# One written order of tasks for all engines in a scan followed by a bilinear feed-forward block

## The chip, the cores and the metric

The kernel runs on one core of one Trainium2 chip. The metric is the time of one execution on the device in microseconds (us); a kernel's figure is the median of its runs. A core has TensorE (matrix products into PSUM, here PE, with PEld for loading its weights), VectorE (DVE), ScalarE (ACT), GpSimd (POOL) and SyncE (SP), which here issues all DMAs from one queue. PSUM has eight banks of 128 partitions x 512 float32.

## What is computed

Four batches, eight heads, 768 positions, head size 32, state size 16. A gated linear recurrence runs along the positions; its result, as 3072 rows of 256, goes through a bilinear feed-forward block with float64 weights:

```
cum = cumsum(log(a)) in the chunk;  L[i,j] = exp(cum[i]-cum[j]) for i >= j, else 0
y[i]  = sum_j (C[i].B[j]) L[i,j] x[j]  +  (C[i].state) exp(cum[i])
state = exp(cum[last]) state + sum_j exp(cum[last]-cum[j]) B[j] x[j]
out   = ((y @ w1) * (y @ w2)) @ w3 @ w_out        # w1, w2: 256x1024, w3: 1024x1024, w_out: 1024x256
```

## The kernel before

**Chunks and slabs.** The positions are cut into 16 chunks of 48; two chunks of all batches are a slab of 384 tokens, eight slabs in all. In a chunk, the 16 groups of two heads lie side by side, the two heads on partition halves 0 to 63 and 64 to 127; the first 16 rows of a half stand for the carried state, the other 48 for the positions.

**A chunk** (`chunk`, L286) has these steps, each in two halves of eight groups where a digit 0 or 1 follows: `D` (L298) forms the exponents cum[i]-cum[j] with the causal mask as one product of a constant `LD` and a table `RD`, whose rows hold cum as three bf16 parts; `E` (L304) takes exp on ScalarE into `R`; `B` (L309) multiplies B by the last decay on GpSimd; `CB` (L314) forms C.B as 32 products of 96x48 from six bf16 slots (three parts of B against three of C); `M` (L328) multiplies the two on VectorE; `Mx` (L333) multiplies `R` by x in 16 float32 products, which gives y and the new state in one PSUM bank `py`; `Z` (L345) transposes the state and copies it in four pieces into the next chunk's x tile; `hi`, `lo` (L360, L364) split y into two fp32r parts for the next products. Chunk c+1's `Mx` waits for chunk c's `Z`. `load_cum` (L260) fetches the parts of cum from DRAM, where `a.save` (L211) put them after clip, log, scan and three rounding steps. B and C of slabs 1 to 7 are split on ScalarE, VectorE and GpSimd (`split_slab`, L225), written to DRAM and read back slot by slot (`load_pack`, L249); slab 0 uses float32 blocks.

**Weights.** Each block of 128x512 float64 values is loaded (`.D`) into one of four buffers `st` and turned into float32 (`from_f64`, L384): `.A` scales the high words, `.Y` moves one byte per value, `.L` shifts and masks, `.S` shifts and merges. w1 and w2 (eight blocks, 512 columns wide each) are then split into a high and a low fp32r part by `.H` and `.P` (L424). w_out stays float32 (`wof`). w3 and w_out are multiplied into one 1024x256 matrix by float32 products (`w3_item`, L449, tasks `v0` to `v15`), whose result is split by `e` (L475).

**Slabs.** `up` (L487) makes one of eight 128-column pieces of both y @ w1 and y @ w2, two PSUM tiles, six fp32r products each (high-high, high-low, low-high, two halves of the 256 rows). `gate_a` copies the one out on ScalarE, `gate_b` multiplies the other in on VectorE, `gate_hi` and `gate_lo` (L513, L518) split the product on ScalarE and GpSimd. `down` (L523) multiplies 128 tokens by the combined matrix, 24 products; `store_a`, `store_b` copy and write it out.

**Order.** The string `PLAN` (L21) is the order of tasks from the beginning to the end of slab 1's `down`, and all instructions that it issues are kept in that order on their engine; `ON_VECTOR` and `ON_POOL` say which tasks leave ScalarE or VectorE, and `+n` are n filler products on zeros. From slab 2 on a loop (L607) issues the work, with chunk steps of the next slab between the ups, and there only the products keep their order (`mm`, L108). The tail is L633: three downs, copies and stores.

Of the kernel before, what the change touches and what calls it, by code (L numbers as in the profile page):

```python
# [45 lines left out]
ON_VECTOR = """
o0.A o1.Y o2.Y o3.A v0.A v0.Y v11.A v14.A v3.Y v5.A v7.Y v8.Y w0.H w1.Y w2.A w3.H w3.Y w4.A w5.H w6.A w6.H
""".split()
ON_POOL = "s1.rB s1.rC s2.rB".split()

@with_exitstack
def kernel(
# [34 lines left out]
    NGF = 11

    const = ctx.enter_context(tc.tile_pool(name="const", bufs=1))
    work = ctx.enter_context(tc.tile_pool(name="work", bufs=2))
    dram = ctx.enter_context(tc.tile_pool(name="dram", bufs=1, space=bass.MemoryType.DRAM))
    ps_at = ctx.enter_context(tc.tile_pool(name="ps_at", bufs=4, space=bass.MemoryType.PSUM))
    ps_l = ctx.enter_context(tc.tile_pool(name="ps_l", bufs=1, space=bass.MemoryType.PSUM))  # L100


    ordered = [True]

    def ins(i):
        return tc.keep_in_program_order(i) if ordered[0] else i

    def mm(*args, **kw):  # L108
        return tc.keep_in_program_order(nc.tensor.matmul(*args, **kw))  # L109

    def load(*args):
        return ins(nc.sync.dma_start(*args))

    def acopy(*args):
        return ins(nc.scalar.copy(*args))  # L115

    def vtt(*args):
        return ins(nc.vector.tensor_tensor(*args))  # L118

    def vcopy(*args):  # L120
        return ins(nc.vector.tensor_copy(*args))  # L121

    def ptt(*args):
        return ins(nc.gpsimd.tensor_tensor(*args))  # L124

    GF = const.tile([P, NGF, TOK], F32, name="gf")  # L130
    gf_turn = [0]

    def next_gf():
        gf_turn[0] += 1
        return GF[:, (gf_turn[0] - 1) % NGF]

    G8 = NB * HP // 2
    NK = 2 * CPS * 2
    first = GF.rearrange("p a s -> p (a s)")
    C0 = first[:, :NK * G8 * T].rearrange("p (k g t) -> p k g t", k=NK, g=G8)  # L140
    B0 = first[:, NK * G8 * T:NK * (G8 * T + TE)].rearrange("p (k m) -> p k m", k=NK)
    zero = const.tile([P, 512], BF16, name="zero")
    nc.vector.memset(zero, 0.0)
    BN = [const.tile([P, CPS, NB * HP, N], F32, name=f"bn{i}") for i in range(2)]

    NG = NB * HP
    RI, RJ = T, T + 6
    KD = RJ + 3 * NG  # L150
    LD = const.tile([KD, 2, TE], BF16, name="ld")
    RD = const.tile([KD, NG, T], BF16, name="rd")
    ldc = const.tile([KD, 2, TE], F32, name="ldc")
    rdc = const.tile([KD, T], F32, name="rdc")
    rdg = const.tile([KD, NG], F32, name="rdg")
    XE = [const.tile([P, NB * HP, 2 * D], F32, name=f"xe{i}") for i in range(2)]

    NSLOT = 6
    KS = NSLOT * N
    BP = const.tile([KS, NB * HP, CPS, 2, TE], BF16, name="bp")  # L160
    CP = const.tile([KS, NB * HP, CPS, 2, T], BF16, name="cp")


    Q, SQ = P // (NB * H), a.shape[1]
    arkc = work.tile([P, 3, SQ], F32, name="arkc", tag="g", bufs=FT + 1)
    ar, keep, cum = [arkc[:, i] for i in range(3)]
    ct = GF[:, NGF - 1].bitcast(BF16)[:, :3 * SQ].rearrange("p (t s) -> p t s", t=3)
    cd = dram.tile([Q, 2, NG, 3, SQ], BF16, name="cd")

# [8 lines left out]
    @task("k.p")  # L178
    def _():
        def fill(t, pattern, op, value, base, step):  # L180
            ins(nc.gpsimd.affine_select(out=t, in_=t, pattern=pattern, compare_op=op, fill=value, base=base,
                                        channel_multiplier=step))

        ins(nc.gpsimd.memset(keep, 1.0))
        ins(nc.gpsimd.memset(keep.rearrange("p (c t) -> p c t", t=T)[:, :, 0:1], 0.0))
        ins(nc.gpsimd.memset(ldc, 0.0))
        for h2 in range(2):
            fill(ldc[:, h2], [[-1, TE]], ALU.is_ge, -BIG, N, 1)
            fill(ldc[:, h2], [[0, TE]], ALU.is_ge, 1.0, RI + 3 * h2 - 1, -1)
# [5 lines left out]
        fill(rdg, [[3, NG]], ALU.is_ge, 0.0, RJ + 2, -1)

    task("k.C")(lambda: ins(nc.gpsimd.memset(C0, 0.0)))
    task("k.X0")(lambda: ins(nc.gpsimd.memset(XE[0], 0.0)))
    task("k.X1")(lambda: ins(nc.gpsimd.memset(XE[1], 0.0)))
    task("k.L")(lambda: vcopy(LD, ldc))  # L200
    task("k.R")(lambda: vtt(RD, rdc.unsqueeze(1).broadcast_to([KD, NG, T]), rdg.unsqueeze(2).broadcast_to([KD, NG, T]),
                            ALU.add))
    task("a")(lambda: load(ar, a))
    task("a.clip")(lambda: ins(nc.vector.tensor_scalar(ar, ar, 1e-6, 1.0, ALU.max, ALU.min)))
    task("a.ln")(lambda: ins(nc.scalar.activation(ar, ar, AF.Ln)))
    task("a.scan")(lambda: ins(nc.vector.tensor_tensor_scan(cum, keep, ar, 0.0, ALU.mult, ALU.add)))
# [79 lines left out]
    def chunk(c):  # L286
# [59 lines left out]
        def _():  # L346
            if c + 1 == NCH:
                return
# [357 lines left out]
```

## Time and profile before

| | |
|---|---|
| Runs | 325.22, 324.51, 322.70 us; median 324.51 |
| Span of the profiled execution, first to last instruction | 323.5 us (its own time is not given apart from this; the runs stand at -0.8 to +1.7 us from the span) |
| Busy: PE, DVE, ACT, POOL | 92%, 48%, 46%, 36% of the span |
| Mean granted clock of TensorE | 0.968 |
| DMA | 45.31 MB, 26255 packets, of them 7600 under 512 B |
| First `up` | 40.87 us |

The page gives busy times of the engines and 40 slices of the span with busy tenths, granted clock (PEclk, tenths of full speed) and DMA. A group is one kind of instruction: line, engine, operation, written tile <- read tiles, shape, count, then busy time in us, mean ns of one, and the engine's idle time ahead of it with what ended it. A timeline row begins with its start and length in us. Windows give, for a stretch, the busy times of PE, PEld, DVE, ACT and POOL, then clock, DMA share and GB/s. Products of float32 operands appear as two records each.

### The profile page before, as it was taken

The page shows a single profiled execution, that of the slowest core. Times are in us where ns is not written, and L with a number is a line of the kernel's source. Part 1 is how long each engine was busy: PE and PEld are TensorE (multiplying, and loading weights), DVE is VectorE, ACT ScalarE, POOL GpSimd, SP SyncE. Part 2 cuts the span into 40 slices and gives each one's busy share as a digit, 9 for nine tenths or more (in the row PEclk, how much of TensorE's full clock was granted, in tenths as well). Part 3 has the DMA queues.
Part 4 walks back from the last instruction along what each step waited for, and adds up shares of the span by engine and source line. Part 5 has one row for each costly group of instructions (what it writes and reads, how often), then busy time and mean ns, then how long its engine had stood idle before and what let it go on. Part 6 is the DMA issues. An engine that isn't in the chain of part 4 may idle for free. (4 is left out here: it accounts for less than half of the span.)

```text
span 323.5 us, 6505 instructions
## 1 busy us (share of the span) xinstructions
PE 297.9 (92%) x2523; PEld 266.0 (82%) x2523; DVE 156.1 (48%) x288; ACT 147.9 (46%) x279; POOL 117.5 (36%) x142
## 2 busy tenths in 40 slices
PE   8695697887997799899999999999999999999995
PEld 3452587776996599799899999999989999999995
DVE  2879969688871632456331651256035405411210
ACT  4366696677671653343523441453145324422430
POOL 8027358415223272333522341342134304421430
PEclk9899699799999799799999999999999999999999
DMA  7599599997999676844581177129402930001001
GB/s 212 181 307 291 163 272 184 280 243 224 335 207 253 195 138 182 227 140 110 118 156 35 51 151 129 29 54 190 95 21 56 187 79 5 3 16 34 0 4 46
DMA packets 26255, 45.31 MB, mean 140 GB/s; under 512 B 7600, under 2 KB 17200, under 8 KB 25552
## 3 DMA queue, kind: packets, MB, share of 16 engines
q1 hardware_dynamic: 26224, 44.89, 54.3%
q8 instruction: 20, 0.33, 0.4%
q14 instruction: 11, 0.09, 0.1%
HBM read 36.77 MB, written 8.11 MB: 139 GB/s over the span
## 5 line engine op out<-in xcount | busy, mean ns | idle before, releaser
L124 POOL TENSOR_TENSOR g<-gf,g 128x384 fp32r<-128x384 f32 x64 | 66.2, 1037 | 98.0 <-ACT g L115 98.0
L109 PE MATMUL bank<-woh,g 128*128 128x256 f32 x384 | 75.3, 291 | 3.1 <-DVE wol L118 2.2
L118 DVE TENSOR_TENSOR gf<-gf,bank 128x384 f32<-128x384 f32 x48 | 26.5, 552 | 103.6 <-PE bank L109 100.7
L109 PEld LDWEIGHTS bank<-woh,g 128*128 128x128 f32 x384 | 62.4, 196 | 5.1 <-DVE wol L118 2.9
L115 ACT COPY gf<-bank 128x384 f32<-128x384 f32 (+1 forms) x72 | 31.7, 444 | 58.7 <-PE bank L109 50.5
L115 ACT CAST g<-gf 128x384 fp32r<-128x384 f32 x64 | 32.9, 514 | 54.7 <-DVE gf L118 51.7
L109 PE MATMUL bank<-wol,g 128*128 128x256 f32 x192 | 55.2, 287 | 0.0
L109 PE MATMUL bank<-xT,w1h 128*128 128x384 f32 x192 | 52.8, 355 | 0.1
L109 PE MATMUL bank<-xT,w2h 128*128 128x384 f32 x192 | 48.8, 335 | 0.0
L109 PEld LDWEIGHTS bank<-wol,g 128*128 128x128 f32 x192 | 37.6, 196 | 0.0
L109 PE MATMUL bank<-wof,mag 128*128 128x256 f32 x128 | 33.0, 410 | 2.6 <-DVE wof L420 2.6
L109 PEld LDWEIGHTS bank<-xT,w1h 128*128 128x128 f32 x192 | 33.1, 188 | 2.1 <-DVE xT L118 0.4
L109 PEld LDWEIGHTS bank<-xT,w2h 128*128 128x128 f32 x192 | 34.8, 188 | 0.0
L109 PE MATMUL bank<-xT,w1l 128*128 128x384 f32 x96 | 32.2, 335 | 0.0
L109 PE MATMUL bank<-xT,w2l 128*128 128x384 f32 x96 | 32.2, 335 | 0.0
L109 PEld LDWEIGHTS bank<-wof,mag 128*128 128x128 f32 x128 | 25.9, 206 | 7.3 <-DVE wof L420 3.0
L115 ACT COPY st<-st 128x512 uint8<-128x512 uint8 x20 | 27.4, 1370 | 7.6 <-DVE mag L402 7.4
L124 POOL TENSOR_TENSOR R<-bn,R 128x128 f32<-128x128 f32 x32 | 14.7, 478 | 43.3 <-issue 36.5
L124 POOL TENSOR_TENSOR part<-raw,part 128x512 bf16<-128x512 f32 (+1 forms) x14 | 15.9, 1137 | 33.3 <-ACT part L115 33.3
L121 DVE COPY xe<-Z 16x256 f32<-16x256 f32 x60 | 26.8, 447 | 1.1
L109 PEld LDWEIGHTS py<-R,xe 128*64 128x64 f32 x512 | 17.8, 146 | 11.4 <-DVE R L118 4.4
L115 ACT CAST part<-raw 128x512 bf16<-128x512 f32 (+1 forms) x28 | 16.0, 578 | 24.3 <-DMA raw<-in_Bt_dram 10.9
(69 smaller groups left out, 388.7 us busy)
## 6 DMA issues: line engine op xcount, KB each, us to landing
st<-in_w3t_dram SPq DMA_DIRECT2D x16, 512.0 KB
xe<-in_x_dram SPq DMA_DIRECT2D x32, 192.0 KB
st<-in_w_dram SPq DMA_DIRECT2D x8, 512.0 KB
db<-part SPq DMA_DIRECT2D x7, 384.0 KB
bp<-db SPq DMA_DIRECT2D x7, 384.0 KB
st<-in_w_out_dram SPq DMA_DIRECT2D x4, 512.0 KB
bn<-in_Bn_dram SPq DMA_DIRECT2D x8, 256.0 KB
dc<-part SPq DMA_DIRECT2D x7, 288.0 KB
```

What stands on the lines that cost most here:

```text
L109: return tc.keep_in_program_order(nc.tensor.matmul(*args, **kw))
L115: return ins(nc.scalar.copy(*args))
L118: return ins(nc.vector.tensor_tensor(*args))
L121: return ins(nc.vector.tensor_copy(*args))
L124: return ins(nc.gpsimd.tensor_tensor(*args))
```

## The change

Nearly the whole body is rewritten; what is computed stays.

- **Order.** `PLAN` now covers the whole kernel. Each word names a task, its engine (`:S` ScalarE, `:V` VectorE, `:G` GpSimd) and its PSUM banks (`@7,6`); every instruction, loads and stores too, keeps this order on its engine. The loop from slab 2 on is gone. The list has its first up right after the second chunk, runs all eight of slabs 0, 1 and 2 and four of slab 3 while w3 arrives, and has the first down (`d0.2.m`) after the last w3 product. Unsplit products of 28 ups wait in a ring `GS`.
- **Decays.** Chunks 0 and 1: log a is also loaded transposed (`at`), spread over a triangle (`Y0`, `Y1`) and multiplied in with one more float32 product per half, no trip through DRAM. Chunks 2 to 7: as before, with cum as two fp32r parts instead of three bf16. Chunks 8 to 15: no product; cum is loaded broadcast over the partitions (`K`, 393 KB), and `F` and `G` on VectorE or GpSimd subtract cum[j] and add the mask.
- **C.B.** B and C come as float32 blocks laid out on the host, two groups side by side (`bc`, 459 KB per chunk); eight float32 products of K=64, 128x96 on alternating row halves and two banks take the place of 32 bf16 ones, and splitting, writing and reading back the parts is gone.
- **Weights.** w1 and w2 blocks hold 128 columns of both matrices with all 256 rows (eight blocks, 1 KB runs in DRAM), so one block serves one `up`. `.Y` moves 16 bits per value. w_out and w3 blocks are also split by `.H` and `.P`, and w3 @ w_out is made of three fp32r products in place of a float32 one. These split tiles share the space of the ring `FR` of split gates (11 places).
- **Splitting of gates** (`h`, `l`) happens after w3 is done, on ScalarE or VectorE and VectorE or GpSimd by the list. The state copies `Z` go to three engines. x is loaded for all 128 partitions with zero rows (512 KB), so that nothing need be cleared.

Cut to its core (the list shown at its start, around the last w3 product, and at its end):

```diff
-ON_VECTOR = """
-ON_POOL = "s1.rB s1.rC s2.rB".split()
+k.act:S k.zero:V k.rd:G c0.B +7@5 a.D t.D k.tri:G k.R:V w0.D c0.N c1.B c1.N c1.X c0.CB@0,1 k.keep:G c0.X a.clip:V k.ld:G a.ln:S w1.D t.clip:V +1@7
...
+c1.lo:V w1.S:V l0.0.m@7,6 w1.H:S w4.D w5.A:S w1.P:V l0.0.a:S w5.Y:V l0.1.m@2,5 w5.L:V c2.N w7.A:V w5.S:V w7.Y:S l0.0.g:V l0.1.a:S w5.H:S w7.L:V w2.D
...
+l3.7.a:S v16.M@2,5 l3.7.g:V l3.5.m@3,4 c11.F0:V c11.F1:G l3.5.a:S c11.G0:G v17.M@2,5 l3.5.g:V c11.G1:V l3.6.m@0,6 e11.a:S@5 l0.2.h:V l0.3.h:V
+e10.a:S@2 l0.0.h:V e11.b:V@5 l0.3.l:G l0.1.h:S e10.b:V@2 l0.5.h:S l0.0.l:G l0.6.h:S l3.0.m@7,1 l0.7.h:S l1.4.h:S l0.4.h:V l0.1.l:V l1.6.h:S l0.5.l:V
...
+l7.1.m@7,4 l7.6.g:V l7.6.h:S l7.1.a:S l7.6.l:G l7.1.g:V l7.1.h:V l7.1.l:V d7.1.m@0 d7.2.m@1 d7.1.y:S d7.1.x d7.0.m@6 d7.2.y:V d7.2.x d7.0.y:S d7.0.x
+    NGS, NST, NMAG, NFR, NOB, NCT, NR, NPK = 28, 4, 5, 11, 2, 2, 2, 3
+    pin = tc.keep_in_program_order
+            def build(e, hf):
+                lc = la[:, c, hf * HG:(hf + 1) * HG]
+                tt(e, Y(hf), lc.unsqueeze(2).broadcast_to([P, HG, T]), tri.unsqueeze(1).broadcast_to([P, HG, T]), ALU.mult)
+            def decay(hf, i):
+                mm(psum[i][:, :HG * T], LD[:k].rearrange("p h m -> p (h m)"), RD[:k, gs].rearrange("p g s -> p (g s)"),
+                   start=True, stop=c >= CPS)
+                if c < CPS:
+                    mm(psum[i][:, :HG * T], XT[:, 0], GS[:, 2 * c + hf], start=False, stop=True)
+            def diff(e, hf):
+                tt(e, ct[:, gs], ct[:, gs], CJ[:, c, gs].unsqueeze(2).broadcast_to([P, HG, T]), ALU.subtract)
+            def causal(e, hf):
+                tt(e, ct[:, gs], ct[:, gs], mask.unsqueeze(1).broadcast_to([P, HG, T]), ALU.add)
+        @step("CB")
+            for k in range(4):
+                for r in range(2):
+                    rows = slice(64 * r, 64 * r + 64)
+                    mm(psum[b[r]][:, 2 * T * k:2 * T * (k + 1)], bq[rows, k, :P], bq[rows, k, P:], start=True, stop=True)
-            b = v["st"].bitcast(U8).rearrange("p (k e) -> p k e", e=8)
-            (vcopy if name + ".Y" in ON_VECTOR else acopy)(b[:, :, 4], b[:, :, 3])
+            h = v["st"].bitcast(U16).rearrange("p (k e) -> p k e", e=4)
+            copy(e, h[:, :, 2], h[:, :, 1])
+        from_f64(f"w{j}", [(i * KT * P, KT * P, (w1, w2)[i][:, 2 * P * j:2 * P * (j + 1)].rearrange("(k p) c -> p k c", p=P))
+                           for i in range(2)], lambda flat=flat: flat(W12[0]), lambda flat=flat: flat(W12[1]))
+                terms = ((0, 0),) if whole else ((0, 0), (0, 1), (1, 0))
+                for n, (l, r) in enumerate(terms):
+                    mm(po, vt[:, l, fs], wt[:, r, kt], start=(kt == KS[0] and f % 2 == 0 and n == 0),
+                       stop=(kt == KS[-1] and f % 2 == 1 and n == len(terms) - 1))
+            for ft in range(FT):
+                for k, (l, r) in enumerate(((0, 0), (0, 1), (1, 0))):
+                    mm(v["p"], vs[ft]["g"][:, l, ts_], WO[:, ft, r], start=(ft == 0 and k == 0),
+                       stop=(ft == FT - 1 and k == 2))
+    for word in PLAN.split():
+        name, _, banks = word.partition("@")
+        name, _, engine = name.partition(":")
+        b = [int(i) for i in banks.split(",")] if banks else []
+            tasks.pop(name)(engine, b)
-    for sl in range(2, NSL):
-        plan = [[] for _ in range(FT + NTT + 1)]
```

More of the change, by code (lines that the diff above doesn't have):

```diff
@@ L130 @@
[L130 to L168, printed above, removed]
+    ps = ctx.enter_context(tc.tile_pool(name="ps", bufs=1, space=bass.MemoryType.PSUM))
@@ new lines, in act, with ring @@
+    def act(*args, **kw):
+        pin(nc.scalar.activation(*args, **kw))
+    psum = [ps.tile([P, 512], F32, name=f"ps{i}") for i in range(8)]
+    turns = {}
+    def ring(name, n):
+        turns[name] = turns.get(name, -1) + 1
+        return turns[name] % n
+    GS = sb([P, NGS, TOK], F32, "gs")
+    FR = sb([P, NFR * 2 * TOK], F32R, "fr")
+    zero = sb([P, 512], BF16, "zero")
+    RI, RJ = T, T + 4
+    KD = RJ + 2 * NG
+    LD = sb([KD, 2, TE], F32R, "ld")
+    RD = sb([KD, NG, T], F32R, "rd")
@@ L170 @@
+    OB = [sb([P, DM], F32, f"ob{i}") for i in range(NOB)]
+    W12 = [sb([P, FT, 2, KT, P], F32R, f"w{p}") for p in "hl"]
+    WO = sb([P, FT, 2, DM], F32R, "wo")
+    Q = P // (2 * NG)
+    cd = dram.tile([SQ // T, Q, 2, NG, T], F32, name="cd")
+    cq = dram.tile([Q, 2, NG, 2, SQ], F32, name="cq")
     tasks = {}
@@ L195, in _ @@
[L195 to L204, printed above, removed]
@@ L372, in chunk @@
-        return [first, second, steps[:1], steps[1:]]
-    for c in range(2 * CPS):
-        task(f"c{c}.X")(lambda c=c: load_x(c))
-        task(f"c{c}.K")(lambda c=c: load_cum(c))
-        for stage in chunk(c):
-            tasks.update(stage)
-    W12 = [[const.tile([P, KT, DF], F32R, name=f"w{i}{p}") for p in "hl"] for i in (1, 2)]
-    WO = [const.tile([P, FT, DM], F32R, name=f"wo{p}") for p in "hl"]
-    def from_f64(name, src, dst=None):
+                        g = n * HP + 2 * kt + pp
@@ L390, in from_f64, with _ @@
+        sv = slice(cc * T, (cc + 1) * T)
+        hi, lo = xT[sl % 2]
+        step("hi")(lambda e, b: copy("S", hi[:, :, :, sv], v["py"][:, :, :, N:]))
+        step("lo")(lambda e, b: tt("V", lo[:, :, :, sv], v["py"][:, :, :, N:], hi.bitcast(F32)[:, :, :, sv],
+                                   ALU.subtract))
+    for c in range(NCH):
+        chunk(c)
+    def from_f64(name, pieces, hi, lo, whole=False):
         v = {}
         @task(name + ".D")
-        def _():
-            v["st"] = work.tile([P, 2 * GR], F32, name="st", bufs=4)
-            load(v["st"].bitcast(U32).rearrange("p (f k) -> p f k", f=src.shape[1]), src)
+        def _(e, b):
+            v["st"] = ST[ring("st", NST)]
+            for lo_c, n, src in pieces:
+                d = v["st"].bitcast(U32)[:, 2 * lo_c:2 * (lo_c + n)]
+                load(d.rearrange("p (f k) -> p f k", f=src.shape[1]), src)
@@ L584, with _ @@
-    for name in PLAN.split():
+        def _(e, b):
+            m = v["mag"].bitcast(U32)
+            d = hi().bitcast(U32) if whole else m
+            pin(nc.vector.scalar_tensor_tensor(d, m, 3, v["wh"].bitcast(U32), ALU.logical_shift_left, ALU.bitwise_or))
+        if whole:
+            return
+        @task(name + ".H")
+        def _(e, b):
+            v["hi"], v["lo"] = hi(), lo()
+            copy(e, v["hi"], v["mag"])
+        task(name + ".P")(lambda e, b: tt(e, v["lo"], v["mag"], v["hi"].bitcast(F32), ALU.subtract))
```

745 lines of the change are left out of this document (347 added, 398 removed).

## The prediction

> **What bounds the kernel now.** I read the totals first, then the stages, then the chain. The page's head and its slices:
>
> ```profile
> span 323.5 us, 6505 instructions
> PE 297.9 (92%) x2523; PEld 266.0 (82%) x2523; DVE 156.1 (48%) x288; ACT 147.9 (46%) x279; POOL 117.5 (36%) x142
> ...
> PE   8695697887997799899999999999999999999995
> ...
> PEclk9899699799999799799999999999999999999999
> DMA  7599599997999676844581177129402930001001
> GB/s 212 181 307 291 163 272 184 280 243 224 335 207 253 195 138 182 227 140 110 118 156 35 51 151 129 29 54 190 95 21 56 187 79 5 3 16 34 0 4 46
> ```
>
> TensorE is the busiest engine, but the two halves differ: to about slice 17 (141 us) it has gaps, a lowered clock and nearly full DMA; after that nothing but matmuls. The windows say it in us:
>
> ```profile
> 0.00:100.00 100.00, 84.18 (x531) 64.54 (x532) 76.80 (x131) 63.33 (x93) 43.57 (x54) 0.93 0.86 241
> ...
> 141.40:319.85 178.45, 177.95 (x1670) 168.50 (x1668) 60.67 (x124) 65.57 (x144) 56.11 (x68) 1.00 0.35 75
> ```
>
> Columns: stretch, length, busy PE, PEld, DVE, ACT, POOL, granted clock, DMA share, GB/s. The second stretch is slabs 2 to 7; only less matmul work would shorten it. So the change is worth what it takes out of the first 141 us. The prices at full clock come from starts in the timeline of TensorE:
>
> ```profile
> 86.49 3.62 PE L109 MATMUL bank<-wof,mag 128*128 128x256 f32 x16
> 89.76 0.70 PE L109 MATMUL pl<-xT,w1h 128*128 128x384 f32 x2
> ...
> 146.42 0.69 PE L109 MATMUL pc<-cp,bp 96*64 96x48 bf16 x32
> 147.04 0.62 PE L109 MATMUL bank<-xT,w1h 128*128 128x384 f32 x2
> ...
> 149.33 1.15 PE L109 MATMUL py<-R,xe 128*64 128x64 f32 x32
> 150.41 0.62 PE L109 MATMUL bank<-xT,w1h 128*128 128x384 f32 x2
> ...
> 152.60 0.51 PE L109 MATMUL bank<-xT,w1h 128*128 128x384 f32 x2
> ...
> 154.68 0.50 PE L109 MATMUL pd<-rd,ld 102*128 102x384 bf16 x2
> 154.89 0.66 PE L109 MATMUL bank<-xT,w1h 128*128 128x384 f32 x2
> ...
> 163.41 0.28 PE L109 MATMUL bank<-woh,g 128*128 128x256 f32 x1
> ...
> 166.27 0.51 PE L109 MATMUL bank<-woh,g 128*128 128x256 f32 x2
> ```
>
> One `up` (12 matmuls) is 154.68 - 152.60 = 2.08 us; one `down` (24) 166.27 - 163.41 = 2.86, so 0.119 each; a float32 matmul of 256 columns, two records, 3.27/8 = 0.41; a chunk's products 1.08 (`Mx`, 1.3 with its lead-in), 0.62 (C B), 0.2 (two decays). Slabs 2 to 7 by these: 48 x 2.08 + 18 x 2.86 = 151.3, leaving 27 for ten chunks, 2.7 each.
>
> In the first stage the same work is late:
>
> ```profile
> 26.65 1.15 PE L109 MATMUL py<-R,xe 128*64 128x64 f32 x32 [0.51 <-DMA xe<-in_x_dram]
> ...
> 34.99 1.98 PE L109 MATMUL py<-R,xe 128*64 128x64 f32 x32 [4.00 <-DVE R L118]
> ...
> 40.87 0.79 PE L109 MATMUL pl<-xT,w1h 128*128 128x384 f32 x2
> ```
>
> The first `up` starts at 40.87. Up to 141.4 TensorE does 16 ups (33.3), 6 downs (17.2), w3 (64 x 0.41 = 26.2), six chunks (16) and fillers: about 93 of useful work in 141 us, 48 lost.
>
> **The change, part by part.** *Start of the first up.* Before, chunk 0's decays waited for cumulative sums to go to DRAM and back. Afterwards chunks 0 and 1 multiply log a (loaded transposed) by an on-chip triangle. The latest input becomes x of chunk 0: nine loads, 3.0 MB by their shapes, in the order of the list. The first 20 us of now, with waits in SP's queue, and a full queue give
>
> ```profile
> 0.00:20.00 20.00, 16.19 (x53) 8.73 (x54) 12.13 (x24) 8.82 (x9) 6.98 (x21) 0.91 0.68 206
> ...
> 25.00:31.00 6.00, 3.75 (x45) 1.58 (x43) 5.93 (x7) 3.70 (x8) 5.54 (x6) 1.00 1.03 283
> ```
>
> 3.0 MB at 283 GB/s is 10.6; with about 2.5 of issue and first latency, 13. Then `MX` of chunk 0 (2, as at 34.99, the clock being lower after gaps), transpose and carry (0.45 + two queued copies of 0.45), `MX` of chunk 1 (2), `hi` and `lo` (0.5 + 0.55), and about 0.5 of handing over: 7. **First up at 20**; bounds 17 (full clock, 330 GB/s) and 27 (x at 206 GB/s, the mean of the first 20 us). w1 and w2 by column tile mean that this up needs one 512 KB block, not four; only the first blocks gate, the rest is below.
>
> *The weight stage, first up to the last w3 product.* The list gives TensorE 28 ups here (58.2), all w3 (16 x 12 x 0.119 = 22.9, since w3 and w_out are split into two fp32r parts and three products cost 0.36 where one float32 one cost 0.41), six `MX` (7.8), seven C B (7), 12 decays (2.4), nine fillers (2): 100. VectorE's load is read from the rows of its first 100 us:
>
> ```profile
> L420 DVE SCALAR_TENSOR_TENSOR mag<-mag,st 128x512 uint32<-128x512 uint32 x24 | 21.4, 892 | 0.3
> L414 DVE TENSOR_SCALAR st<-st 128x512 int32<-128x512 int32 x28 | 16.2, 578 | 7.7 <-ACT st L115 7.4
> L121 DVE COPY st<-st 128x512 uint8<-128x512 uint8 x8 | 8.6, 1072 | 1.2 <-ACT mag L404 1.2
> ...
> L118 DVE TENSOR_TENSOR gf<-gf,pl 128x384 f32<-128x384 f32 x11 | 6.0, 547 | 0.6 <-ACT gf L115 0.5
> L402 DVE TENSOR_SCALAR mag<-st 128x512 f32<-128x512 f32 x9 | 4.8, 538 | 2.3 <-DMA st<-in_w_out_dram 1.7 <-DMA st<-in_w3t_dram 0.5
> ...
> L118 DVE TENSOR_TENSOR raw<-raw,part 128x512 f32<-128x512 f32 x1 | 0.7, 693 | 0.0
> ```
>
> Counted in the list: 26 `S` x 0.892 = 23.2; 26 `L` x 0.578 = 15.0; 7 `Y` x 1.07 = 7.5; 12 `A` x 0.538 = 6.5; 13 `P` x 0.69 = 9.0; 27 gates x 0.55 = 14.9; 16 `M`, 6 `lo` and 10 decay steps of late chunks x 0.55 = 17.6; small ones (5 `H`, 6 `T`, 8 carries, 2 splits) about 11. Sum 104. `Y` now moves 16-bit pieces; no row shows that, bounds 0.43 (the quickest `L`, below) and 1.07, and I keep 1.07 as the nearest row. By counts ScalarE has some 72 here, GpSimd 45. **VectorE (104) and TensorE (100) bound the stage almost together**, in two fixed queues that wait for each other: a late gate on VectorE holds a PSUM bank, and the up behind it waits. For that I add 6; bounds 0, and 23 (VectorE's idle time in the first 100 us of before). Last product at 20 + 104 + 6 = **130**. DMA must land 25.8 MB by the last weight block: 91 us at 283 GB/s, so it is not the bound unless it drops under 220.
>
> What contention with GpSimd costs VectorE stands in VectorE's timeline, the same instruction alone and beside it (with the quickest `L` ahead):
>
> ```profile
> 8.54 0.43 DVE L414 TENSOR_SCALAR st<-st 128x512 int32<-128x512 int32 x1
> ...
> 9.84 0.68 DVE L420 SCALAR_TENSOR_TENSOR mag<-mag,st 128x512 uint32<-128x512 uint32 x1
> ...
> 26.05 1.53 DVE L420 SCALAR_TENSOR_TENSOR mag<-mag,st 128x512 uint32<-128x512 uint32 x1
> ```
>
> In the second GpSimd was 5.54 of 6.0 us busy (the window above). The 892 is the mix. [...]
>
> *From the last w3 product on.* 36 ups (74.9), 24 downs (68.7), eight `MX` (10.4), six C B (6): **160**. C B as float32 blocks has no row: eight matmuls of 96 columns per chunk. By the 256-column float32 row (1.6 ns a column) 8 x 96 is 1.23; by `Mx` (16 matmuls of 64 columns in 1.08, column halves in turn, 1.05 ns a column) 0.81. I take 1.0: here row halves alternate as column halves do there. Over 16 chunks the bounds are 3 below and 4 above. Chunks 8 to 15 drop their two decays (8 x 0.2, in the count) and pay 32 instructions of 0.55 on VectorE or about 1 on GpSimd:
>
> ```profile
> L124 POOL TENSOR_TENSOR g<-gf,g 128x384 fp32r<-128x384 f32 x64 | 66.2, 1037 | 98.0 <-ACT g L115 98.0
> ```
>
> Of these 64 subtractions 34 move to VectorE. After 130 VectorE has about 78 and GpSimd 51 to do, beside TensorE's 160: costed at nothing. If that cover went, 1 us per late slab would be 7. The broadcast decay loads (3.1 MB) lie where the DMA share was 0.35. On SP's queue the output stores wait for their copy with loads of the next chunks behind them; those are due a slab later.
>
> *Stalls I can name.* Gates of slab 0 are split only once the ring that shares the w3 space is free: between that and the first down each of VectorE, ScalarE and GpSimd has some 7, TensorE three ups and an `MX` (7.6): 2 lost. At the end, the list computes up 7.1 last, but `down` still takes ft in the order 0, 1, ...: its second part waits for copy, product, cast and subtraction of 7.1, 0.44 + 0.55 + 0.42 + 0.55 and handing over, 2.2. Then the tail, as now from the last matmul on:
>
> ```profile
> 319.85 0.04 issue
> 319.88 0.37 ACT gf L115
> ```
>
> 323.5 - 319.85 = 3.65.
>
> **Sum:** 20 + 110 + 160.2 + 2 + 2.2 + 3.65 = 298. Against this execution's span, 323.5, it is 25.5 less. The median of the three runs, 324.51, is 1.0 above that span, so the forecast for a median is **299 us**.
>
> **The rivals.** *1. Dense from the start.* VectorE sheds contention (its best durations, 0.69 for `S`, 0.43 for `L`, give 87), TensorE bounds the stage at 100, C B costs 0.81: 20 + 99 + 159 + 8 = 286. For it: the stage has many independent ups. Against: both queues are in one fixed order.
>
> *2. Blocks come late.* w1 and w2 come in 1 KB pieces, four staging buffers turn over, and one SP queue holds loads behind any wait. If the first 100 us again give 206 to 241 GB/s, 25.8 MB take 107 to 125; with 2.5 ahead and 15 for converting and multiplying the last, the last product is at 125 to 143, end 293 to 311, and with lost clock 313. Against: the many loads under 2 KB of split B and C are gone.
>
> [...]
>
> *4. Given back later: no change.* The ring of split gates has 11 places, a slab's downs hold 8; if each later slab waits 3.5 for splitting, 7 x 3.5 takes the gain: 322. Against: three ups (6.2) normally stand between.
>
> **How the numbers follow.** Forecast 0.60 (289 to 309), rival 1 0.13, rival 2 0.15, rival 4 0.06, rival 3 0.06. A measurement of this kernel can tell about 1% from no change (321.3 to 327.8). Faster: 0.60 + 0.13 + 0.15 = 0.88; same 0.06; slower 0.06. The range goes from just under the dense case (284) to just short of rival 4 (320), which takes in 27 for the first up and 23 of coupling one at a time; it leaves out rivals 3 and 4 and the lower part of rival 1.
>
> **What would show it.** Right: first up near 20, last w3 product near 130, no TensorE gap over 2 us later except before the last downs, `S` near 0.9. Wrong: a first up after 27; VectorE under 80% busy between 20 and 130 while TensorE waits (then DMA or order binds); C B over 1.3 per chunk; a steady slab longer than its ups and downs plus 2.3 per chunk. A last product after 160 makes the whole forecast wrong.

## The result, and the profile after

The kernel after takes 295.05 us (median of 4 runs, 295.01 to 296.45), the kernel before beside it 324.87: a ratio of 0.910, 95% interval 0.906 to 0.914. The forecast was 299 in 284 to 320. Some executions begin with TensorE at about half rate (1.65 us for a product that takes 0.91) and take 6 to 7 us longer (three of four in experiment 7, one of five in experiment 8, by the profile of one of each); the times below are those of the others. The page of the profiled execution (295.09 us, span 293.4):

```profile
span 293.4 us, 6102 instructions
...
PE 280.5 (96%) x2360; PEld 263.7 (90%) x2360; DVE 187.6 (64%) x347; ACT 121.2 (41%) x236; POOL 113.4 (39%) x157
...
PE   7898999999999996999999999999999999999985
...
DVE  4557898987999999789453848086245943540520
...
PEclk9999999999999999999999999999999999999999
DMA  7976995959684574403164010087013100001001
```

TensorE's gaps and lowered clocks are nearly gone from the first half: between the fifth slice and the last two only one, the 16th (110 to 117 us), is below 9. VectorE, busy for 48% of the span before, is now at seven tenths or more from the 4th slice to the 19th. The stages, in windows cut at the first `up`, the last w3 product, the first `down` and the last product (columns as in the prediction):

```profile
0.00:20.62 20.62, 17.63 (x148) 9.45 (x148) 10.18 (x25) 6.97 (x12) 14.01 (x43) 1.00 0.88 306
...
20.62:126.90 106.28, 101.06 (x845) 95.30 (x844) 93.31 (x169) 63.39 (x110) 47.51 (x53) 1.00 0.66 219
...
126.90:136.10 9.20, 9.20 (x79) 8.88 (x78) 9.04 (x13) 6.43 (x15) 8.20 (x7) 1.00 0.27 92
136.10:289.90 153.80, 152.63 (x1295) 150.09 (x1293) 75.06 (x144) 44.06 (x99) 43.72 (x54) 1.00 0.21 61
```

The cuts come from TensorE's timeline:

```profile
4.43 1.16 PE L131 MATMUL ps<-bc 64*128 64x96 f32 x16
...
8.42 0.91 PE L131 MATMUL ps<-gs,xt 128*128 128x384 f32 x2
...
14.26 0.81 PE L131 MATMUL ps<-zero 128*128 128x512 bf16 x3
15.00 1.15 PE L131 MATMUL ps<-r,xe 128*64 128x64 f32 x32
...
19.55 1.14 PE L131 MATMUL ps<-bc 64*128 64x96 f32 x16
20.62 0.97 PE L131 MATMUL ps<-xT,wh 128*128 128x384 f32 x2
...
111.45 1.15 PE L131 MATMUL ps<-r,xe 128*64 128x64 f32 x32 [1.42 <-ACT gs L143]
...
116.20 0.45 PE L131 MATMUL ps<-xT,wh 128*128 128x384 f32 x1 [0.90 <-DVE xT L137]
...
125.26 1.60 PE L131 MATMUL ps<-fr 128*128 128x256 f32 x12
126.69 0.51 PE L131 MATMUL ps<-xT,wh 128*128 128x384 f32 x2
...
136.30 8.71 PE L131 MATMUL ps<-wo,fr 128*128 128x256 f32 x72
...
217.82 2.03 PE L131 MATMUL ps<-bc 64*128 64x96 f32 x32
219.78 3.11 PE L131 MATMUL ps<-wo,fr 128*128 128x256 f32 x24
...
279.85 0.51 PE L131 MATMUL ps<-wo,fr 128*128 128x256 f32 x3
281.12 8.80 PE L131 MATMUL ps<-wo,fr 128*128 128x256 f32 x69 [0.76 <-DVE fr L143]
```

The first `up` starts at 20.62 instead of 40.87. All w3 is multiplied by 126.9, with 27 ups done, and by 136.3 there are 31 (64.5 us by the prediction's price); the kernel before had 16 ups and 6 downs (50.5) behind it at 141.4. (The prediction counts 28 ups up to the last w3 product, and the description of the change counts four of slab 3; the list has `l3.6.m` right behind that product.) In the prediction's prices the useful work of TensorE up to 126.9 is 27 ups 56.2, w3 22.9, eight `MX` 8.6, ten C B 10, decays 6: 104, so 23 us are lost where before lost 48. That is 25 of the 30 us; the rest is a few us less work.

### The profile page after: what moved, and what is told of

It is laid out like the page before. It is cut to its first block, busy times and chain, and to the rows that moved or that the text cites. A ratio compares the mean times of both kernels' runs of the same rounds, so it can differ in the third digit from the quotient of the medians.

```text
span 293.4 us, 6102 instructions
## 1 busy us (share of the span) xinstructions
PE 280.5 (96%) x2360; PEld 263.7 (90%) x2360; DVE 187.6 (64%) x347; ACT 121.2 (41%) x236; POOL 113.4 (39%) x157
## 4 chain that ended last, share of the span: by engine, by line
PE 65%; DVE 15%; issue 5%; DMA 5%; ACT 5%; SPq 1%; POOL 1%; DVEq 0%; ACTq 0%; POOLq 0%
PE ps L131 65%; DVE mag L440 3%; DVE st L140 3%; DMA st<-in_w_dram 2%; DMA xe<-in_x_dram 2%; ACT st L143 2%; DVE gs L137 2%; DVE st L143 2%; DVE mag L140 1%; DVE ct L137 1%; SPq L134 1%; DMA st<-in_w3t_dram 1%; DVE r L137 1%; ACT gs L143 1%; ACT mag L146 1%
## 5 line engine op out<-in xcount | busy, mean ns | idle before, releaser
L131 PE MATMUL ps<-xT,wh 128*128 128x384 f32 x512 | 132.1, 337 | 2.0 <-DVE xT L137 1.1
L131 PEld LDWEIGHTS ps<-xT,wh 128*128 128x128 f32 x512 | 91.1, 188 | 4.2 <-DVE xT L137 2.0
L131 PE MATMUL ps<-xT,wl 128*128 128x384 f32 x256 | 85.9, 336 | 1.6 <-POOL wl L137 1.2
L131 PE MATMUL ps<-wo,fr 128*128 128x256 f32 x576 | 71.6, 282 | 0.8 <-DVE fr L143 0.8
L131 PEld LDWEIGHTS ps<-wo,fr 128*128 128x128 f32 x576 | 69.8, 188 | 1.6 <-DVE fr L143 1.0
L137 DVE TENSOR_TENSOR gs<-gs,ps 128x384 f32<-128x384 f32 x64 | 34.7, 548 | 38.4 <-PE ps L131 36.2
L137 POOL TENSOR_TENSOR fr<-gs,fr 128x384 fp32r<-128x384 f32 x30 | 33.3, 1128 | 61.9 <-DVE fr L143 28.0
L131 PEld LDWEIGHTS ps<-xT,wl 128*128 128x128 f32 x256 | 48.1, 188 | 2.2 <-POOL wl L137 1.5
L143 ACT COPY gs<-ps 128x384 f32<-128x384 f32 x64 | 31.2, 494 | 44.6 <-PE ps L131 44.5
L131 PE MATMUL ps<-fr 128*128 128x256 f32 x192 | 26.1, 285 | 0.3 <-DVE fr L137 0.3
```

The costliest lines, as they stand in the source:

```text
L131: pin(nc.tensor.matmul(*args, **kw))
L137: pin((nc.gpsimd if e == "G" else nc.vector).tensor_tensor(*args))
L143: pin(nc.scalar.copy(*args) if e == "S" else (nc.gpsimd if e == "G" else nc.vector).tensor_copy(*args))
```

## The experiments

Three readings were set against each other. **A**: TensorE and VectorE bind the weight stage together, VectorE its second half, and whatever moves the start moves the end. **B**: the gain is TensorE's cheaper work (three fp32r products for a float32 one, fewer decays, C B in blocks). **C**: the arrival of weight blocks sets the pace. Each kernel is the kernel after with one edit; its "last cast" is the start of ScalarE's `e11` cast right behind the last w3 product, at 126.89 us in the kernel after. Intervals are those of the ratio to the kernel before, beside which each ran.

**1. Less VectorE work.** The seven moves `.Y` on VectorE (w5, v01, v03, v05, v07, v17, o3) are struck from the list, here the first.

```diff
-... l0.0.a:S w5.Y:V l0.1.m@2,5 ...
+... l0.0.a:S l0.1.m@2,5 ...
```

> The changed kernel without the seven 16-bit moves (.Y) that VectorE does; the low bits of seven weight blocks stay unset. VectorE loses 7 x 1.1 = 7.7 us in the weight stage, TensorE nothing. If VectorE binds that stage (theory A), it ends 4 to 6 us earlier: 289 to 291 us, bounded by TensorE's own idle time of some 6 us there. If TensorE binds it (theory B), at most 1 us: 294 to 295. If the arrival of the weight blocks binds it (theory C), no change.

292.01 us, 0.898 (0.893 to 0.904): 3.0 less than after, with the last cast at 123.95, 2.9 earlier. 7.7 us of VectorE work (seven moves of 1.105) give 3 us. That is 1 us short of A's 289 to 291 and 2 us beyond B's 294.

**2. Less TensorE work.** w3's products use the high parts alone.

```diff
-                terms = ((0, 0),) if whole else ((0, 0), (0, 1), (1, 0))
+                terms = ((0, 0),)
```

> The changed kernel with w3 @ w_out made of the high parts alone, one product where three stand; the low parts are still made and not used. TensorE loses 128 products of 0.119 = 15.3 us in the weight stage, the other engines nothing. Theory A (VectorE binds): 3 us or less, 292 to 295. Theory B (TensorE binds): 10 to 15 us, 280 to 285. Theory C (blocks bind): no change. Both in one fixed order, coupled: between, about 289.

292.28 us, 0.901 (0.894 to 0.908), last cast 123.99. 128 products of 0.119, 15.2 us of TensorE work, give 2.8. The windows of the stage's second half, first of the kernel after:

```profile
80.00:100.00 20.00, 19.74 (x144) 19.25 (x142) 19.09 (x35) 13.51 (x24) 7.60 (x7) 1.00 0.56 190
100.00:120.00 20.00, 17.35 (x184) 16.46 (x183) 19.20 (x33) 10.01 (x21) 10.69 (x13) 1.00 0.67 218
```

and of this one:

```profile
80.00:100.00 20.00, 17.42 (x124) 15.93 (x124) 19.18 (x35) 13.15 (x24) 7.07 (x7) 0.91 0.58 188
100.00:120.00 20.00, 15.01 (x135) 14.20 (x131) 19.17 (x33) 10.02 (x22) 10.72 (x13) 0.91 0.64 211
```

The relieved TensorE idles (17.4 and 15.0 of 20) and even gets a lower clock (0.91 for 1.00), while VectorE stays at 19.2 of 20. From 80 us on it is VectorE's order, and not TensorE's work, that sets the pace. B in its plain form falls; A stands, within limits that experiments 6 and 10 set.

**3. The w3 split undone.** One float32 product per block pair, on the high part's tile read as float32; the `.P` steps of w3 and w_out go.

```diff
-                    mm(po, vt[:, l, fs], wt[:, r, kt], start=...
+                    mm(po, vt.bitcast(F32)[:, l, fs], wt.bitcast(F32)[:, r, kt], start=...
-                terms = ((0, 0),) if whole else ((0, 0), (0, 1), (1, 0))
+                terms = ((0, 0),)
```

> The changed kernel with w3 @ w_out as one float32 product of the high parts in place of three of fp32r, and without the 20 subtractions (.P) that make the low parts, so the low parts are left out of the result. TensorE gains 64 x (0.41 - 0.36) = 3.4 us in the weight stage, VectorE loses 9 x 0.69 = 6.2 and GpSimd 11 x 1.41 there. Theory A (VectorE binds, TensorE close behind): -2 to +1, 293 to 296. If the split products are a gain by TensorE's time: 298 to 299.

294.94 us, 0.907 (0.904 to 0.910), last cast 126.66: no difference to after. The windows of this kernel show why:

```profile
50.00:100.00 50.00, 50.00 (x338) 46.87 (x336) 37.14 (x74) 30.84 (x54) 11.92 (x17) 1.00 0.69 224
100.00:127.00 27.00, 27.00 (x225) 25.07 (x225) 17.98 (x39) 11.22 (x23) 8.75 (x13) 1.00 0.56 174
```

TensorE is busy all the time from 50 us on and VectorE about 70% of it. TensorE waits for no block there, so C falls. The split makes TensorE's work cheaper (three products 0.36, one float32 product 0.41 in the kernel before) and VectorE's dearer (0.69 a `.P`) by as much as counts: the bound changes its engine and the time stays.

**4. Blocks of 512 columns.** w1 and w2 again as blocks of one matrix, 128 rows by 512 columns; the first ups move behind the four, or eight, blocks that they need.

```diff
-    for j in range(FT):
+    for j, (q, i, kt) in {0: (0, 0, 0), 1: (0, 0, 1), 5: (0, 1, 0), 7: (0, 1, 1),
+                          3: (1, 0, 0), 4: (1, 0, 1), 2: (1, 1, 0), 6: (1, 1, 1)}.items():
...
+        src = (w1, w2)[i][kt * P:(kt + 1) * P, 2 * GR * q:2 * GR * (q + 1)].unsqueeze(1)
```

> The changed kernel with w1 and w2 in blocks of 512 columns of one matrix and one half of the rows, as before the change, so that four blocks must be in before the first up and eight before the fifth; the first ups move behind them in the list, the rest stays. If the early first up is what the stage gains from: first up near 31 in place of 20.6, total 5 to 10 us longer, 300 to 305. If VectorE or the blocks' arrival bind the stage anyway: within 2 us of 295.

312.09 us, 0.960 (0.954 to 0.967), last cast 143.02. 17 us are lost, more than expected. Its TensorE timeline:

```profile
29.78 1.01 PE L131 MATMUL ps<-xT,wh 128*128 128x384 f32 x2 [7.13 <-ACT r L146]
...
52.23 2.01 PE L131 MATMUL ps<-r,xe 128*64 128x64 f32 x32 [5.52 <-DVE r L137]
```

The first up comes 9.2 late. The other 7 lie between there and the last cast, in waits like the second row: the chain to it runs through steps of weight blocks on ScalarE, VectorE and GpSimd that stand ahead of the chunk's steps in the list. After such gaps TensorE is slow as well: between 29.78 and 60 its mean granted clock is 0.79, and this `MX` takes 2.01 where it took 1.15. A list made anew for these blocks could do better, so 17 is at most what the column tiles are worth.

**5. First decays through DRAM.** Chunks 0 and 1 get their cumulative sums as chunks 2 to 7 do.

```diff
-                    mm(psum[i][:, :HG * T], XT[:, 0], GS[:, 2 * c + hf], start=False, stop=True)
...
-            if c >= CPS:
+            if True:
                 @step("K")
```

> The changed kernel with chunks 0 and 1 taking their decays as chunks 2 to 7 do, through DRAM, in place of the triangular product; the DMA queue waits for the saved sums first. If the first up's time goes through to the end: first up at 26 to 28, total 5 to 7 us longer, 300 to 302. If the stage behind absorbs it: within 1.5 us of 295.

304.32 us, 0.936 (0.929 to 0.943): 9.3 more than after. TensorE's timeline:

```profile
16.62 0.98 PE L131 MATMUL ps<-rd,ld 84*128 84x384 f32 x2 [9.00 <-DMA rd<-cq]
...
30.08 0.97 PE L131 MATMUL ps<-xT,wh 128*128 128x384 f32 x2
```

One wait of 9.0 for the table from DRAM, the first up 9.46 later (5 to 7 had been expected), the last cast 9.49 later (136.38), the span 9.5 longer. TensorE's granted clock falls in the wait and is 0.72 in the mean up to the first up, which is part of the 9.46. The start is passed on to the end one to one; nothing behind it has slack to take it up.

**6. Late decays as products.** Chunks 8 to 15 get `D0` and `D1` on TensorE again; `F` and `G` go (chunk 8's words shown).

```diff
-DIRECT = 8
+DIRECT = 16
-... c5.D1@2 c5.D0@1 c9.K v03.M@3,7 c8.F0:V ...
-... c6.Z0:S l2.7.m@1,6 c8.E0:S ...
+... c6.Z0:S c8.D0@1 c8.D1@6 c9.K l2.7.m@0,3 c8.E0:S ...
```

> The changed kernel with the decays of chunks 8 to 15 as products again, as chunks 2 to 7 have them (their loads move behind the decays of the chunk before). TensorE gains 16 x 0.18 = 2.9 us, VectorE loses 16 instructions of about 0.86 (ten of them in the weight stage, 8 us), GpSimd 16 of about 1.0. Theory A (VectorE binds the weight stage, TensorE the rest): the stage ends 2 to 3 us earlier, the rest takes 2.2 longer: 293.5 to 296. If putting late decays on VectorE is itself a gain: 297 to 299, TensorE's 2.9 in full.

298.13 us, 0.918 (0.914 to 0.922), 3.1 more than after. The last cast is 0.75 earlier (126.14), and the stretch from there on is 3.6 longer. This is the second reading's 297 to 299; A's 293.5 to 296 failed, for VectorE was busy 7.9 us less in the weight stage (85.4 of 105.5) and the stage ended 0.75 earlier and not 2 to 3. Taking these products away is a gain, since from 127 us on TensorE alone binds.

**7. Row halves in turn or not.** C B with the four products of the upper row half first, then the four of the lower.

```diff
-            for k in range(4):
-                for r in range(2):
+            for r in range(2):
+                for k in range(4):
```

> The changed kernel with the eight C B products of a chunk in another order: four on the upper row half, then four on the lower, in place of turns. If products on different halves overlap, one chunk's C B goes from 1.07 to 1.2 or 1.3 us, and the ten or so chunks' worth that lie on TensorE's path add 1.5 to 3: 296.5 to 298. If they do not overlap (1.07 is 8 products one after the other): no change, 294.5 to 295.5.

297.29 us, 2.2 more, from one run; the other three took 304.4 to 304.7, and the profiled one of these began with TensorE at half rate, which is told of in the last section. Two chunks in a row, in its timeline:

```profile
226.75 2.71 PE L131 MATMUL ps<-bc 64*128 64x96 f32 x32
229.40 3.10 PE L131 MATMUL ps<-wo,fr 128*128 128x256 f32 x24
```

2.65 / 2 = 1.33 a chunk, against 1.96 / 2 = 0.98 between 217.82 and 219.78 of the kernel after. With the halves in turn a chunk's products take 0.35 less, an overlap in part, as the prediction took it. Six of the 16 chunks have their C B behind the weight stage, where TensorE alone binds; 6 x 0.35 = 2.1 would be the 2.2. The profile, though its first up is 8.3 late, bears this out in part: from the last cast (134.79) to the end it is 1.7 us longer than the kernel after.

**8. All `l` on GpSimd**, as `gate_lo` before; two of them:

```diff
-... l5.3.l:V l5.5.l:V ...
+... l5.3.l:G l5.5.l:G ...
```

> The changed kernel with all 64 subtractions of split gates (.l) on GpSimd, as before the change; VectorE loses 34 x 0.79 = 27 us, all after the weight stage, GpSimd gains 34 x 1.04 = 35 there. As forecast (these cost nothing beside TensorE): later slabs unchanged, but before the first down eight stand in one row on GpSimd where two engines shared them, 2 to 4 us: 297 to 299. If sharing matters in every slab (eight in a row, 8.3 us, against the ups between): 2 us or more per slab, 308 or more.

297.62 us, 0.915 (0.912 to 0.919): 2.6 more, as forecast, but not in the forecast place. Ahead of the first down TensorE loses nothing (9.23 of 9.23 us busy from the last cast on); it waits for GpSimd later, longest inside a down of slab 5:

```profile
245.22 2.88 PE L131 MATMUL ps<-wo,fr 128*128 128x256 f32 x22 [1.32 <-POOL fr L137]
```

This and a wait in the last downs (0.58) make 1.9; in this profile, one of an execution that began at half rate, the stretch from the last cast to the end is 2.1 longer. Sharing these subtractions is worth some 2 us.

**9. No fillers.** All words `+n` are struck, here the first.

```diff
-k.act:S k.zero:V k.rd:G c0.B +7@5 a.D t.D ...
+k.act:S k.zero:V k.rd:G c0.B a.D t.D ...
```

> The changed kernel without its 30 filler products on zeros (21 of them ahead of the first up). If the fillers buy TensorE's clock for the chain of the first two chunks (two of the runs seen had that chain at half speed, 1.65 us for a product that takes 0.91, and ended 6 to 7 us later): first up at 26 to 28, 300 to 303. If they only fill time in which TensorE waits: first up unchanged or a little earlier, 293 to 295.

300.74 us, 0.925 (0.919 to 0.932): 5.7 more. Its first decay and first up:

```profile
8.71 1.65 PE L131 MATMUL ps<-gs,xt 128*128 128x384 f32 x2
...
25.95 1.01 PE L131 MATMUL ps<-xT,wh 128*128 128x384 f32 x2
```

The decays take 1.65 instead of 0.91, the first up is 5.3 later and the last cast 5.7 (132.56), as expected. The fillers, products on zeros, are worth 5.7 us here: with them the chain to the first up runs at full rate (0.91 for the decay product). They are no part of the change, though: the kernel before has 43 ahead of its first up.

**10 and 11. The moves elsewhere.** The seven `.Y` of VectorE go to ScalarE (shown), or to GpSimd; in both kernels `down` also takes its parts in the order of 12.

```diff
-... w5.Y:V ... v01.Y:V ...
+... w5.Y:S ... v01.Y:S ...
```

> The changed kernel, complete, with the seven 16-bit moves of VectorE given to ScalarE (1.38 us each, 61 of 96 us busy in the weight stage), and the downs taking their parts in the order in which the last slab's ups are made, 7.1 last. VectorE binds the stage: as light_v, -3, if ScalarE's queue has room in the right places; the last down no longer waits 0.8: -0.8. Together 291 to 293. If ScalarE's order gets in the way: 294 or more.

> The same as y_act with the seven moves on GpSimd (1.48 us each, 43 of 96 us busy there). If GpSimd's idle time is free: 291 to 293. [...]

294.77 us (its quickest two 294.04), 0.908 (0.901 to 0.914), and 296.78 us, 0.912 (0.906 to 0.917). Beside kernel 12, which differs from them in the moves alone, that is 0.5 to 1.2 (intervals overlapping, so none is shown) and 3.2 more. The expected gain did not come, and GpSimd's time is above its expected 291 to 293; the last casts are at 127.21 and 130.35, against 126.62 in kernel 12. What became of it stands in VectorE's step `L`, which follows the move; first with ScalarE, then with GpSimd:

```profile
L140 DVE TENSOR_SCALAR st<-st 128x512 int32<-128x512 int32 x26 | 14.5, 568 | 9.1 <-ACT st L143 9.1
...
L140 DVE TENSOR_SCALAR st<-st 128x512 int32<-128x512 int32 x26 | 16.2, 631 | 10.1 <-ACT st L143 5.1 <-POOL st L143 4.9
```

In kernel 12 VectorE waits 5.2 ahead of `L`; now it waits 4 to 5 us more, for the moves that it gave away (in the kernel after ScalarE takes 1.378 for one, GpSimd 1.479). With GpSimd its own instructions grow too: `S` 0.736 for 0.698, `L` 0.631 for 0.567, `P` 0.767 for 0.692, together 3.4 us. With 1 and 6 this limits theory A. Some 8 us less on VectorE moved the last cast by 2.9 where the moves were left out, by 0.75 where the late decays went, and not forward at all here. Only the first also shortens the chain of a weight block (`A`, `Y`, `L`, `S`, `H`, `P`, product). So this chain seems to set the stage more than VectorE's sum does; no run separates the two further.

**12. The parts of `down` in the order of the gates.**

```diff
-            for ft in range(FT):
+            fts = [2, 4, 0, 7, 5, 3, 6, 1]
+            for ft in fts:
                 for k, (l, r) in enumerate(((0, 0), (0, 1), (1, 0))):
-                    mm(v["p"], vs[ft]["g"][:, l, ts_], WO[:, ft, r], start=(ft == 0 and k == 0),
-                       stop=(ft == FT - 1 and k == 2))
+                    mm(v["p"], vs[ft]["g"][:, l, ts_], WO[:, ft, r], start=(ft == fts[0] and k == 0),
+                       stop=(ft == fts[-1] and k == 2))
```

> The kernel after with one edit and nothing left out: every down takes its eight parts in the order in which the last slab's gates are made, 2, 4, 0, 7, 5, 3, 6, 1, instead of 0 to 7. If the wait inside the last downs (0.8 us by the profile after) is a wait for the gate of up 7.1 that lies on the path to the end, it goes, and the downs of the last slab stand as 72 products in a row: 293.9 to 294.4 us against 295.05, a ratio to before that is 0.002 to 0.004 lower than that of the kernel after. If the wait only moves into the downs (a later part is late instead), the time stays at 294.8 to 295.3.

293.55 us (293.43 to 294.84, 6 runs), 0.906 (0.901 to 0.910): 1.5 less than after. Its last downs:

```profile
279.59 8.70 PE L131 MATMUL ps<-wo,fr 128*128 128x256 f32 x72
```

All 72 products stand in a row, 0.121 each, where the kernel after had three, a wait and 69 in 8.80, and they end 1.6 us earlier. This is the quickest complete version that was run; its ratio's interval overlaps that of the kernel after, but all six of its runs lie below all four of after.

## Why the prediction was right, and where its terms were off

| Term | Predicted | Measured |
|---|---|---|
| First up | 20 | 20.62 |
| From there to the end of the last w3 product | 110 | 106.3 |
| From there to the last product | 160.2 + 2 + 2.2 = 164.4 | 163.0 |
| Tail | 3.65 | 3.5 |
| Span | 298 | 293.4 |

*First up.* The number is right, the wait named for it is not, and two errors cancel: `MX` of chunk 0 came at 15.0 and not 13, and it took 1.15 and not 2, since TensorE ran at its full rate (1.15 is also what `MX` takes at 111.45). x of chunk 0, the named wait, was issued at 5.09 and took at most 6.9 to land, so it was there by 12.0. `MX` stood behind the decay products of both chunks and three fillers (the row at 14.26), with no idle time just ahead of it. Without fillers the first up came at 26.0, inside the upper bound of 27 (experiment 9), without the triangle at 30.1, beyond it (experiment 5).

*The weight stage.* The step "VectorE (104) and TensorE (100) bound the stage almost together", with 6 for waiting on each other, was right in that taking work from either engine gave little (experiments 1 to 3). TensorE was busy 101.1 of 106.3 us, and its idle 5.2 answers to the 6. Its 100 should have been 98, for the list has 27 ups here and not 28. VectorE's term was mis-sized: it was busy 93.3, not 104. Of its 17 groups between 20.62 and 126.9:

```profile
L440 DVE SCALAR_TENSOR_TENSOR mag<-mag,st 128x512 uint32<-128x512 uint32 x27 | 18.4, 697 | 0.1
...
L140 DVE TENSOR_SCALAR st<-st 128x512 int32<-128x512 int32 x26 | 14.5, 567 | 5.3 <-ACT st L143 5.2
...
L143 DVE COPY st<-st 128x512 uint16<-128x512 uint16 x7 | 7.7, 1105 | 0.0
...
L137 DVE TENSOR_TENSOR ct<-ct,cj 128x384 f32<-128x384 f32 x6 | 5.7, 962 | 0.0
```

`S` took 0.697, not 0.892: 4.8 us less. The 0.892 of before was a mean of instructions alone (0.68) and beside GpSimd (1.53), and in the new list `S` seldom meets GpSimd: 7 of the 27 lie beside a GpSimd instruction for 0.3 us or more, and the longest of them takes 0.90. The first step of the late decays took 0.962, not 0.55: 2.5 more. The 16-bit `Y`, kept at 1.07 from the byte move, took 1.105. All 17 groups add up to 103.4, close to the 104. The 10 us lie in the adding: VectorE's timeline has

```profile
35.70 1.28 DVE L440 SCALAR_TENSOR_TENSOR mag<-mag,st 128x512 uint32<-128x512 uint32 x2
...
41.43 0.68 DVE L440 SCALAR_TENSOR_TENSOR mag<-mag,st 128x512 uint32<-128x512 uint32 x1
```

Two in a row take 1.28, not 1.36 to 1.4: the records of neighbours overlap, by 0.06 in the mean over 169 instructions (103.4 - 93.3). TensorE's terms, made from start to start, don't have this error, VectorE's durations do. So the stage was predicted from an engine that stood idle for 13 of its 106.3 us, and what adds up is TensorE's 101.1 + 5.2. That 104 + 6 came within 4 us of it is in part luck.

*Contention* of VectorE with GpSimd did not carry the last w3 product past 130 (126.9), yet it is there. In the stage `S` mostly escapes it (0.697 in the mean, 0.68 alone) and others do not. A move `Y` alone, one beside GpSimd, and GpSimd's own instruction at that time:

```profile
59.28 0.73 DVE L143 COPY st<-st 128x512 uint16<-128x512 uint16 x1
...
73.68 1.90 DVE L143 COPY st<-st 128x512 uint16<-128x512 uint16 x1
...
73.48 1.49 POOL L143 COPY st<-st 128x512 uint16<-128x512 uint16 x1 [0.71 <-ACT mag L146]
```

The means of `L`, `Y` and `A` (0.567, 1.105, 0.609) lie above their medians (0.43, 0.76, 0.42); over 26, 7 and 12 instructions that is 8 us, an estimate of what these lost if all of it is contention. Behind the w3 stage the same subtraction of split gates runs on both engines at once; VectorE's timeline, beside GpSimd and later alone:

```profile
129.37 5.24 DVE L137 TENSOR_TENSOR fr<-gs,fr 128x384 fp32r<-128x384 f32 x4
...
199.25 1.01 DVE L137 TENSOR_TENSOR fr<-gs,fr 128x384 fp32r<-128x384 f32 x2
```

GpSimd's timeline at the same place:

```profile
127.23 8.25 POOL L137 TENSOR_TENSOR fr<-gs,fr 128x384 fp32r<-128x384 f32 x7 [2.64 <-DVE fr L143]
```

Alone one takes VectorE 0.51 (1.01 / 2), beside GpSimd 1.31 (5.24 / 4): it is held up by 0.80, most of one of GpSimd's 1.18 (8.25 / 7). Yet the two do not run one after the other: in the 5.24 us GpSimd did 4.4 of its own (5.24 / 1.18), whose shortest in this kernel takes 1.00, and in turns the two would have needed 4 x 0.51 + 4.4 x 1.00 = 6.4. So the rows give what such a pair costs here; what that costs a stage is a matter of how often the list sets such a pair side by side.

*Late decays at nothing, C B at 1.0.* Both right: the first covered by TensorE's 163 us (experiment 6), the second 0.98 (1.07 with what comes before and after it, 19.55 to 20.62). The serial price, 1.33 in experiment 7, lies above the bound of 1.23.

*Stalls.* Here 3 us too much was taken. Ahead of the first down TensorE lost nothing: 9.20 of 9.20 us busy between 126.9 and 136.1. The prediction let three ups and an `MX` (7.6) stand there; the list has four (9.6). In the last downs it lost 0.9 (from 279.85 + 3 x 0.12 to 281.12) and about 0.5 more among the 69 (8.80 - 69 x 0.121), not 2.2: the copy of 7.1's first tile runs while its second is multiplied. Experiment 12 takes that away and gains 1.5. Against these 3 stand 1.6 of work more than counted (161.8 busy for 160.2): the list has 37 ups behind the last w3 product, not 36, which makes the 160.2 into 162.3. So the 164.4 is near 163.0 because a miscount and two stalls taken too dear cancel.

*The rivals.* Rival 1 had half of its condition: VectorE's 93.3 (87 in the rival) lies below TensorE's 101, though not without contention. The 20 + 99 did not follow, since TensorE still lost 5.2 in waits for other engines. Rival 2 did not come: the longest idle times of the stage are put down to engines (1.20, 1.42 and 0.90 ahead of TensorE at 28.64, 111.45 and 116.20, 5.2 ahead of VectorE's `L`), none of these to a DMA. DMA moved 219 GB/s, just under the 220 that the prediction named, but with a share of 0.66 it was not full. Rival 3, the case of a last w3 product after 160, did not come: it ended at 126.9. Rival 4 did not come: TensorE is busy 152.63 us of the 153.80 from the first down to the last product. Of the signs of being right, `S` near 0.9 failed (0.697); the others came, the longest gap of TensorE behind 126.9 other than in the last downs being 0.32.

*What the change is made of.* By taking one part away at a time: column tiles up to 17, first decays on the chip 9.3, late decays off TensorE 3.1, sharing of `l` 2.6, row halves in turn 2.2 (one run), the w3 split 0; fillers, which both kernels have, 5.7. These overlap and don't add up to the 30, above all the column tiles, the first decays and the fillers, which all bring the first up forward. Left open: the written order itself, for no run gave the new parts the old loop; what column tiles are worth with a list made for wide blocks; and the old path of B and C through splitting and DRAM, which was not put back.

## What to carry to other kernels

When a long stage behind is dense on one engine, work out first when that engine gets its first real work: what the first up lost was passed on to the end here (5.3 us became 5.7, 9.5 stayed 9.5), and each of the three things that concern it (no trip through DRAM, one small block for the first product, fillers ahead of the chain) weighs more than any change to the products that was taken away (0 to 3.1). Where two engines bind a stage together, taking work from one of them buys little (15 us of TensorE bought 2.8, 7.7 us of VectorE 3.0), and moving work to an engine that is idle on the mean can lose: VectorE then waited 4 to 5 us for the moves that it had given away. Make the consumer take its parts in the order in which they are made: one line gave 1.5 us.

## What the hardware showed that was not expected

**The rate at the start.** In the profiled execution of experiment 7 the first chain ran at about half rate although its fillers stood where those of the kernel after do:

```profile
4.39 2.99 PE L131 MATMUL ps<-bc 64*128 64x96 f32 x16
...
10.17 1.65 PE L131 MATMUL ps<-gs,xt 128*128 128x384 f32 x2
```

1.65 against 0.91 for the same product in the kernel after, and its first up at 28.91, later even than without fillers (25.95). The granted clock in the profile's rows reads 1.00 here, so the durations tell of the rate and the row does not. In the profiled execution of experiment 8 the row shows it too. There the first C B ran at full rate (1.14), then TensorE waited 1.56 for GpSimd, and after that:

```profile
9.81 1.65 PE L131 MATMUL ps<-gs,xt 128*128 128x384 f32 x2
...
8.00:20.00 12.00, 12.00 (x33) 5.33 (x32) 5.08 (x11) 3.22 (x5) 4.31 (x8) 0.50 0.92 340
```

The granted clock is 0.50 and the first up comes at 26.85. Executions of one kernel thus lay 6 to 7 us apart (297.29 and 304.4, 297.6 and 303.79). By the durations the product took 1.8 times as long (1.65 / 0.91). Seven fillers stand ahead of the first C B in both, as in the kernel after (1.26 to 4.43 there), where the chain ran at full rate; what decides between the two rates was not shown, and more fillers were not tried. The 6 to 7 us are 2% of the span, because the chain to the first up hangs on it (28.91 and 26.85 for 20.62).

**A move of 16 bits cost as much as one of 8.** 1.105 us against 1.072 on VectorE and 1.378 against 1.370 on ScalarE, for 512 values per partition. VectorE's means include moves beside GpSimd (up to 1.90 and 2.22); the shortest are 0.732 and 0.741.
